# Block-recurrent cross attention and SwiGLU on one core: batch 0's exponentials transposed unnormalised, read states turned one batch later, orders dealt anew

## The chip, the core and the metric

The kernel runs on one core of a Trainium2 chip. A core has five engines, each of which works through its own list of instructions in order: PE (TensorE, matrix products and transposes), DVE (VectorE), ACT (ScalarE), POOL (GpSimd) and SP (SyncE, which here only issues DMA transfers). They share an on-chip buffer, SBUF, and PE writes its results to PSUM, a small accumulator memory of eight banks, from which another engine reads them. Engines wait for each other by semaphores.

The metric is the device time of one execution in microseconds, the median of several runs. What can be told from no change is about 0.2%.

## The reference

Everything is float32. Attention between tokens `x` (8 batches, 8 heads, 512 tokens, 64 wide) and a small `state` (32 rows per head) runs both ways, and a feed-forward network follows over the 512 + 32 rows of each batch:

```python
scores = x @ state.T / 8                 # per batch and head: 512 x 32
a = exp(scores - scores.max(-1)); a /= a.sum(-1) + 1e-9
xread = a @ state                        # 512 x 64
scores2 = state @ x.T / 8                # 32 x 512
a2 = exp(scores2 - scores2.max(-1)); a2 /= a2.sum(-1) + 1e-9
sread = a2 @ x                           # 32 x 64
x = concatenate([xread, sread])          # heads side by side: (8 * 544) x 512
xn = x / sqrt(mean(x * x) + 1e-6) * rms_g
out = (silu(xn @ w_gate) * (xn @ w_val)) @ w_out      # 512 -> 1536 -> 512
```

## The kernel before

**The fold.** `xread` is never formed for the tokens. Since `xn @ w` is (a times state) times w, the kernel multiplies each head's state with the weights first (`own_weights`, L708: products at L721, copies to SBUF as `v` at L733), and the FFN's first product becomes `v` against the transposed attention weights `aT_s`. The mean square that the norm needs comes from the same weights: in batch 0 through the Gram matrix of the state, later from the squares of the read (L447, L457). `mean_root` (L306, on POOL) turns it to the inverse root `ri`, `along_rows` (L312, transposes at L316) lays `ri` along the tokens, and a DVE product puts it into `aT_s`.

**Batches.** Batch 0's tokens take the plain products: `hidden` (L753) for each of twelve blocks m of 128 hidden columns, 128x512 with two contraction steps for the gate and two for the value, then silu on ACT and the gated product on DVE, then `project_as_ready` (L964). From batch 1 on, products go by a seven-product scheme over halves: `hidden_seven` (L858, products at L868) and `project_twice` (L1141, products at L1172, copies of parts `kept` at L1185, their sums on DVE L1212 and POOL L1200 to L1205, stores at L1288). They take sums of `v` (`vs`, POOL L748 to L751) and of `aT_s` (`aT_t`, `slot_sums`, L782). The 256 state rows of all batches come last, from the collected `xsT`.

**Softmax of batch 0.** It goes in two halves of 256 tokens. `half_read` (L540) sums the exponentials, divides by the sum, transposes the result to `aT_s` (PE L555, ACT L558), forms the Gram product (L562), multiplies it with `aT_s` (L566), sums over partitions with a product by a column of ones (L571), and scales by `ri`.

**The read of the states.** `states_read` (L602) does the second softmax. For batches 2 and later its exponentials go through DRAM and come back transposed; PE forms the read `rp` (L656, small tiles 128*32, bank `at`), ACT scales it to `sr` (L672), PE transposes `sr` (L675), and ACT copies that to `xsT` (L677).

**What sets the order.** Each part is a Python generator, a stream, and a string of letters says which stream takes its next step: `ORDER` for batch 0, `FIRST` for batch 1, `PERIOD` for batches 2 to 6, `LAST` for batch 7, `STATES` for the end. The instructions of all five engines are then in exactly that order. In the later strings `a` is the next batch's `tokens_read`, `s` its `states_read`, `w` its first `own_weights` products, `x` copies of `v`; `h`, `t`, `u` are the hidden products, their copies and sums; `p`, `c`, `k`, `o` are the projection's products, copies, sums and stores; `f`, `g`, `l` are loads. So near the end of each period, the next batch's softmax is finished among the projection's products. I call that place the seam.

**PSUM.** The banks are in pools: `aps` (two, name `at`), `vps` (two, `pv`), `fx` (two), `fy` and `fz` (one each, all named `f`). A product must wait until the last reader of the bank that it takes is done.

Some products use a part of PE's array (the profile's 64*32, 128*32 and 32*64 behind the name); the text calls runs of them small-tile groups, and the others dense.

Of the kernel before, what the change touches and what calls it, by code (L numbers as in the profile page):

```python
# [8 lines left out]
F32 = mybir.dt.float32  # L9
# [5 lines left out]
ALU = mybir.AluOpType  # L15
# [11 lines left out]
    "zzzzaazagaaigaagaazzzebzaaaaabgdabbebbeessbbbzaaddsbbbAeAaadbAaabdAbbeAAAadbAAAb"  # L27
    "aabvdbbevvedAhteeieeAAAhuhtAddssddssppihvvivupAssAAdssshssAAtpseeeddhushedspeedd"
    "AAAApAAdAtvvvhhhuptuheeeddpppeeeddhdvtueeAApeAAdvvedddpAAASdAAeedhtedhuhtvAvvpSS"
    "SAAApSSSSSehuehthAAeeeehuAeppSddpdddvdvvhtudSSkkkkkhkkQkkkQQhhttphQQQuuQQQppppck"  # L30
    "kQQQcAApcwwwwwwwwpwcSS"
# [3 lines left out]
    "vhhththtuhhhuthutataaaaaahhthhluhuxhxxhvvuuuhttuthhhxxxxxthxhhuuauuhaaftauukkktk"  # L35
    "htthhhvauutuuahththxxxhthaaauaahhhhuuuutttasuhhthhhppusuuuauutuauuhukkkkgukaappp"
    "pppskpcppppppppkkkkkfffckkkkakkgpcakkaaakpppcosagaggggspppppppapppapcssckkkaakkk"
    "kaaaaasssoppppkoolaappkppkppppsaapappkkkkoaafwsswcpssfxxsxpcoowxxox"
# [3 lines left out]
    "hahtqqtavaxqaaxhthahhahuuvvtqhuuhthttqxxxqhqqqquGhhhuutxquhhuqafthathhatxxaxuhhq"  # L42
    "qquuhtuhqththhthhuukukkuutvkxxuuahtthaaahhhaafxsthuuuutsuhthahhtuuuuaahhtuuthupp"
    "hsssauaGffpgppcpppGluukukkkpckkppkkkkppkpkkkapapppppaacppppkckkpppakpppagakaaacp"
    "ggsskppaaaookpgkkaakpakagkkckkaoopasppklpkpkpksssppaasfpppasskooappcssawwgwxxfxx"
    "xxpcoo"
)
LAST = (
    "vhhtfthhthxuhguxhtvvhutuhxfhtuthuhhuhhxtuthfxhtuxtxuhxhuhuvtauhhhthxuuthkxthuhhh"
    "kuututxhxtkhuhhthuuuuhututhhhutuhhutguuthukpuphuuukpppkpkgpckpkppkkakppkppkppkpc"  # L50
    "pkakpppkpkckpkkkpakpcppkkacpopppppppakcokkpkpkkkgppkappapkggkakpppppcfopkopgcooo"
    "ao"
# [8 lines left out]
def kernel(  # L61
# [124 lines left out]
    VE.memset(blocks, 0.0)  # L186
    for j in range(4):
        VE.memset(blocks[Ns * j:Ns * j + Ns, Ns * j:Ns * j + Ns], 1.0 / DM)

# [350 lines left out]
    def half_read(h):  # L540

        eS, aT = soft_0["e"][:, HT * h:HT * h + HT], aT_s[0][:, :, HS * h:HS * h + HS]
        e = eS.rearrange("p c e j n -> p (c e j) n")
        z = soft_0["z"][:, HT * h:HT * h + HT].rearrange("p c k -> p (c k)")
        VE.reduce_sum(out=z, in_=e, axis=AXX)
        yield
        VE.tensor_scalar(z, z, 1e-9, None, op0=ALU.add)
        VE.reciprocal(z, z)
        yield
        VE.tensor_tensor(out=e, in0=e, in1=z.unsqueeze(2).to_broadcast(e.shape), op=ALU.mult)  # L550
        yield
        tp = aps.tile([P, 2, HT, P], F32, name="at")
        for i in range(2):
            for c in range(HT):
                TE.transpose(out=tp[:, i, c, :], identity=ident,  # L555
                             in_=eS[:, c, i].rearrange("p j n -> p (j n)"))
        yield
        SE.copy(aT, tp.rearrange("p e c t -> p e (c t)"))  # L558
# [24 lines left out]
        yield  # L583
# [18 lines left out]
    def states_read(b):  # L602
# [48 lines left out]
        rp = aps.tile([P, 2, D], F32, name="at")  # L651
# [21 lines left out]
        yield  # L673
        tp = aps.tile([P, 4, Ns], F32, name="at")
        TE.transpose(out=tp.rearrange("p j n -> p (j n)"), in_=sr, identity=ident)  # L675
# [77 lines left out]
    def hidden(m, lhs, rhs):  # L753
# [6 lines left out]
        def products():  # L760
            for k, to in enumerate((gp, vp)):
# [571 lines left out]
    soft_0["z"] = two.tile([P, NC, 2 * 4], F32, name="z1")  # L1333
    aT_s[0] = two.tile([P, 2, S], F32, name="aT_s")
# [20 lines left out]
    with tc.manual_schedule(**by_hand):  # L1355
# [7 lines left out]
        for b in range(1, B):  # L1363
# [56 lines left out]
```

## Time and profile before

| | |
|---|---|
| median of 3 runs | 741.5 us (741.49 to 742.0) |
| the profiled execution | 741.17 us, of which the span of instructions is 739.1 us |
| PE, DVE, ACT, POOL busy | 99%, 77%, 50%, 36% of the span |
| granted PE clock | 1.0 |
| mean DMA rate | 198 GB/s |

A row of the timeline reads: start, length, engine and line, operation, out<-in, tile of PE's array, shape and number of records; in brackets the idle time ahead of it and what ended it. PE writes two records for most float32 matmuls, and one for a transpose. Ends of PE's records are modelled and overlap the next start, so the distance between starts is the better price. A row of the windows reads: stretch, its length, then for PE, weight loads, DVE, ACT and POOL the busy time and the number of instructions, then PE's clock, the share of DMA time and GB/s.

### The profile page before, as it was taken

To read this page: it belongs to the slowest core of one execution; us is meant where nothing else is said; L and a number is where in the kernel's file an instruction comes from. 1 tells how busy PE (TensorE), PEld (TensorE's weight loads), DVE (VectorE), ACT (ScalarE), POOL (GpSimd) and SP (SyncE) were. 2 spreads that over 40 slices of the span, in tenths; PEclk is the share of its full clock that TensorE was granted. 3 is DMA by queue.
4 is the path that set the end of the run, shared out by engine and by line. 5 is a ranking of instruction groups with operands and counts; after the bars stand their busy time and mean duration, and the time that the engine had idled before them with its cause. 6 is when DMAs were issued, how large, how long until landed. Compare 5 with 4: busy or idle time off the path is not lost.

```text
span 739.1 us, 14234 instructions
## 1 busy us (share of the span) xinstructions
PE 732.8 (99%) x5588; PEld 589.5 (80%) x5588; DVE 565.9 (77%) x943; ACT 367.5 (50%) x620; POOL 264.6 (36%) x360
## 2 busy tenths in 40 slices
PE   8999999999999999999999999999999999999998
PEld 7543444889878997799888987899779987899996
DVE  5775577999848994699569984899569955788862
ACT  5997843563365526472366336552557236511220
POOL 2300004512474127412761247412741277325400
PEclk9999999999999999999999999999999999999999
DMA  8978846973782478418870768238840873063411
GB/s 238 371 279 317 339 175 255 300 279 104 220 308 58 179 255 287 135 34 312 264 242 6 279 202 316 60 147 276 298 131 21 322 228 112 1 226 116 137 51 28
DMA packets 58426, 146.15 MB, mean 198 GB/s; under 512 B 10228, under 2 KB 29176, under 8 KB 51448
## 3 DMA queue, kind: packets, MB, share of 16 engines
q1 hardware_dynamic: 47312, 126.30, 48.1%
q10 hardware_dynamic: 11048, 18.95, 9.0%
q8 instruction: 44, 0.72, 0.4%
q14 instruction: 22, 0.18, 0.1%
HBM read 116.46 MB, written 28.77 MB: 197 GB/s over the span
## 4 chain that ended last, share of the span: by engine, by line
PE 73%; DVE 19%; issue 3%; ACT 2%; POOL 2%; DVEq 0%; POOLq 0%
PE f L868 37%; PE f L1172 10%; PE f L971 6%; PE pv L764 6%; PE pv L721 4%; PE at L721 3%; PE f L1034 2%; DVE hb L1231 2%; DVE h L1220 2%; DVE h L1222 2%; DVE h L1226 2%; DVE sq L457 2%; DVE kept L1212 1%; PE at L656 1%; DVE h L1224 1%
## 5 line engine op out<-in xcount | busy, mean ns | idle before, releaser
L868 PE MATMUL f<-aT_s,v 128*128 128x256 f32 x504 | 119.0, 382 | 0.0
L868 PEld LDWEIGHTS f<-aT_s,v 128*128 128x128 f32 x504 | 94.7, 190 | 22.7 <-issue 5.3
L931 DVE TENSOR_TENSOR g<-g,f 128x512 f32<-128x512 f32 x84 | 55.9, 684 | 60.5 <-PE f L868 51.1
L1200 POOL TENSOR_TENSOR kept<-kept 128x256 f32<-128x256 f32 x28 | 22.7, 810 | 194.1 <-DVE kept L1212 180.6
L1185 ACT COPY kept<-f 128x512 f32<-128x512 f32 (+1 forms) x56 | 29.7, 531 | 119.8 <-PE f L1172 93.8
L868 PE MATMUL f<-aT_t,vs 128*128 128x256 f32 x336 | 86.8, 382 | 0.0
L1172 PE MATMUL f<-w,h 128*128 128x128 f32 x588 | 74.9, 277 | 0.0
L868 PEld LDWEIGHTS f<-aT_t,vs 128*128 128x128 f32 x336 | 62.9, 190 | 13.5 <-issue 2.8
L1172 PEld LDWEIGHTS f<-w,h 128*128 128x128 f32 x588 | 70.0, 192 | 4.1 <-issue 4.1
L922 ACT ACTIVATE hb<-g 128x1024 f32<-128x1024 f32 x42 | 44.5, 1060 | 50.6 <-DVE g L931 50.3
L748 POOL TENSOR_TENSOR vs<-v 128x256 f32<-128x256 f32 x42 | 31.1, 740 | 97.3 <-ACT v L733 97.1
L944 DVE TENSOR_TENSOR hb<-hb,f 128x512 f32<-128x512 f32 (+1 forms) x48 | 31.1, 649 | 23.7 <-PE f L868 23.7
L971 PE MATMUL f<-wo,hb 128*128 128x512 f32 x96 | 44.1, 599 | 0.0
L944 DVE TENSOR_TENSOR hb<-hb,c 128x512 f32<-128x512 f32 (+1 forms) x48 | 37.6, 782 | 8.3 <-ACT hb L922 7.3
L764 PE MATMUL pv<-aT_s,v 128*128 128x512 f32 x96 | 43.9, 597 | 0.0
L868 PE MATMUL f<-aT_t,v 128*128 128x256 f32 x168 | 43.7, 382 | 0.0
L868 PE MATMUL f<-aT_s,vs 128*128 128x256 f32 x168 | 43.1, 379 | 0.0
L1172 PE MATMUL f<-wo,h 128*128 128x128 f32 x336 | 42.1, 275 | 0.0
L1172 PE MATMUL f<-wo,hb 128*128 128x128 f32 x336 | 42.1, 275 | 0.0
L1172 PEld LDWEIGHTS f<-wo,hb 128*128 128x128 f32 x336 | 40.3, 192 | 0.4
L309 POOL TENSOR_TENSOR ri<-ss,mhalf 128x4 f32<-128x4 f32 (+1 forms) x9 | 9.7, 1078 | 86.1 <-ACT ss L397 71.6
L1172 PEld LDWEIGHTS f<-wo,h 128*128 128x128 f32 x336 | 39.8, 192 | 0.0
(230 smaller groups left out, 1593.1 us busy)
## 6 DMA issues: line engine op xcount, KB each, us to landing
w_m<-w_d SPq DMA_DIRECT2D x48, 1024.0 KB
w<-t_d SPq DMA_DIRECT2D x49, 576.0 KB
out_dram<-kept SPq DMA_DIRECT2D x28, 256.0 KB
raw<-in_moe_w_val_dram SPq DMA_DIRECT2D x6, 1024.0 KB
raw<-in_moe_w_out_dram SPq DMA_DIRECT2D x6, 1024.0 KB
w_d<-w_m SPq DMA_DIRECT2D x6, 1024.0 KB
x_b<-in_x_dram SPq DMA_DIRECT2D x6, 1024.0 KB
x_d<-xB ACTq DMA_DIRECT2D x6, 1024.0 KB
```

The costliest lines, as they stand in the source:

```text
L457: VE.tensor_tensor(out=sq[:, i, :], in0=sq[:, i, :], in1=sq[:, j, :], op=ALU.add)
L721: TE.matmul(out=pv[e][Ns * j:Ns * j + Ns, :], lhsT=stT_g[b][D * e:D * e + D, j, :], rhs=w[D * e:D * e + D, j].rearrange("p m k f -> p (m k ...
L748: GE.tensor_tensor(out=vs[:, 0], in0=a21, in1=a22, op=ALU.add)
L764: TE.matmul(out=to[0], lhsT=lhs(i, k), rhs=r, start=(i == 0), stop=(i == len(rhs) - 1))
L868: TE.matmul(out=ps[:, i, 0:half], lhsT=l[:, i, :], rhs=r, start=(start and i == 0 and k == 0), stop=(k == len(lhs) - 1), skip_group_check= ...
L922: SE.activation(out=hb[:, 2 * mp:2 * mp + 2, 0:n].rearrange("p m (c t) -> p m c t", c=2), in_=q["g"][:, :, :, 0:half], func=ACTF.Silu if s ...
L931: VE.tensor_tensor(out=to, in0=to, in1=q[ps][:, :, 0:half], op=ALU.add)
L944: VE.tensor_tensor(out=part, in0=part, in1=val, op=ALU.mult)
L971: TE.matmul(out=banks[r], lhsT=hb[:, m, P * r:P * r + P], rhs=wo[:, m, :], start=(m == 0), stop=(m == NM - 1))
L1172: TE.matmul(out=to[half][:, slot, :], lhsT=lhs[:, k, :], rhs=rhs[:, k, :], start=(fresh and n in (0, 4) and k == 0), stop=(k == QM - 1), s ...
L1185: SE.copy(of_half(k, i), banks[name][i])
L1200: GE.tensor_tensor(out=k[:, 4:8:3], in0=k[:, 5:6].to_broadcast([P, 2, QD]), in1=k[:, 4:8:3], op=ALU.add)
```

## The change

It has four parts.

1. `half_read` transposes batch 0's exponentials as they are, directly behind the exponential (L549 of the changed file). The sum, its reciprocal and the reciprocal's square `zz` (POOL) are formed beside that; the normalised copy is a new tile `en`. The Gram product and the squares are taken of the unnormalised values; the sums over partitions come out per head (a product with the four columns of `of_head`), are multiplied by `zz` into `qz`, whose ninth column holds 1e-6, and are added up. Then `en` is transposed into the same `aT_s`. For each half this is four PE transposes, one ACT copy, one DVE operation and one POOL operation more. `ri` is laid along the tokens in the bank fz instead of pv.
2. The first block of `hidden` (m = 0) makes its products in token halves: eight of 256 columns instead of four of 512, so that the first four need only the first half of `aT_s`.
3. For batches 2 and later the state's read goes to fz, and the transpose of `sr` with its copy becomes a stream of its own, `states_turned` (letter `n`), in the next batch's string.
4. The strings `ORDER`, `PERIOD`, `FIRST` and `LAST` are new; `STATES` is not.

```diff
 PERIOD = (
-    "vhhththtuhhhuthutataaaaaahhthhluhuxhxxhvvuuuhttuthhhxxxxxthxhhuuauuhaaftauukkktk"
...
+    "vxahthththuhuhuthththhthhvvhaaaxxhhxxafaauuuutttuhhthhaahhuuuuttxhuhhthhauukkath"
...
     def half_read(h):
...
-        VE.reduce_sum(out=z, in_=e, axis=AXX)
-        yield
-        VE.tensor_scalar(z, z, 1e-9, None, op0=ALU.add)
-        VE.reciprocal(z, z)
-        yield
-        VE.tensor_tensor(out=e, in0=e, in1=z.unsqueeze(2).to_broadcast(e.shape), op=ALU.mult)
-        yield
         tp = aps.tile([P, 2, HT, P], F32, name="at")
...
         SE.copy(aT, tp.rearrange("p e c t -> p e (c t)"))
         yield
+        z, zz = (soft_0[k][:, HT * h:HT * h + HT].rearrange("p c k -> p (c k)") for k in ("z", "zz"))
+        VE.reduce_sum(out=z, in_=eS.rearrange("p c e j n -> p (c e j) n"), axis=AXX)
+        yield
+        VE.tensor_scalar(z, z, 1e-9, None, op0=ALU.add)
+        VE.reciprocal(z, z)
+        GE.tensor_tensor(out=zz, in0=z, in1=z, op=ALU.mult)
+        yield
+        en = x_0.tile([P, HT, 2, 4 * Ns], F32, name="en")
+        e = eS.rearrange("p c e j n -> p (c e j) n")
+        VE.tensor_tensor(out=en.rearrange("p c e (j n) -> p (c e j) n", n=Ns), in0=e,
+                         in1=z.unsqueeze(2).to_broadcast(e.shape), op=ALU.mult)
+        yield
         ga = vps.tile([P, 2, HS], F32, name="pv")
...
-        sp = fy.tile([P, HT], F32, name="f")
+        sp = fy.tile([P, HT, 2, 4], F32, name="f")
         for i in range(2):
             for c in range(HT):
-                TE.matmul(out=sp[:, c:c + 1], lhsT=sq[:, i, P * c:P * c + P], rhs=ones,
-                          start=(c == 0 and i == 0), stop=(i == 1), skip_group_check=True)
-        yield
+                TE.matmul(out=sp[:, c, i, :], lhsT=sq[:, i, P * c:P * c + P], rhs=of_head,
+                          start=True, stop=True)
+        yield
+        qz = soft_0["qz"][h]
+        VE.tensor_tensor(out=qz[:, :, 0:2 * 4], in0=sp.rearrange("p c e j -> p c (e j)"),
+                         in1=soft_0["zz"][:, HT * h:HT * h + HT], op=ALU.mult)
         ss = two.tile([P, NC], F32, name="ss")
-        VE.tensor_scalar(ss[:, 0:HT], sp, 1e-6, None, op0=ALU.add)
+        VE.reduce_sum(out=ss[:, 0:HT], in_=qz, axis=AXX)
         yield
         ri = mean_root(ss[:, 0:HT], HT)
         yield
-        rp = along_rows(ri, HT, vps, "pv")
+        tp = aps.tile([P, 2, HT, P], F32, name="at")
+        for i in range(2):
+            for c in range(HT):
+                TE.transpose(out=tp[:, i, c, :], in_=en[:, c, i, :], identity=ident)
+        yield
+        SE.copy(aT, tp.rearrange("p e c t -> p e (c t)"))
+        yield
+        rp = along_rows(ri, HT, fz, "f")
...
-        rp = aps.tile([P, 2, D], F32, name="at")
+        rp = aps.tile([P, 2, D], F32, name="at") if b < 2 else fz.tile([P, 2, D], F32, name="f")
...
+        unturned[b] = sr
+        if b < 2:
+            yield from states_turned(b)
+
+    unturned = {}
+
+    def states_turned(b):
+
         tp = aps.tile([P, 4, Ns], F32, name="at")
-        TE.transpose(out=tp.rearrange("p j n -> p (j n)"), in_=sr, identity=ident)
+        TE.transpose(out=tp.rearrange("p j n -> p (j n)"), in_=unturned.pop(b), identity=ident)
...
         def products():
+            if m == 0:
+                gp.append(vps.tile([P, S], F32, name="pv"))
+                vp.append(vps.tile([P, S], F32, name="pv"))
+                for t in (slice(0, HS), slice(HS, S)):
+                    for k, to in enumerate((gp, vp)):
+                        for i, r in enumerate(rhs):
+                            TE.matmul(out=to[0][:, t], lhsT=lhs(i, k), rhs=r[:, t],
+                                      start=(i == 0), stop=(i == len(rhs) - 1))
+                    yield
+                return
...
+            if b > 1:
+                streams.update(n=states_turned(b))
```

On PE at the start of the program, from the first half's transposes of the exponentials (`eS`) to the first gate products (`pv<-aT_s,v`). Before:

```order
L592 MATMUL at<-xT,apart 32x256 x16
L1312 MATMUL f<-wake 128x256
L555 MATMUL at<-ident,eS 128x128 x4
L327 MATMUL at<-ident,rows 128x128
L562 MATMUL pv<-aT_s,gram 128x256 x2
L555 MATMUL at<-ident,eS 128x128 x4
...
L316 MATMUL pv<-ident,ri 128x128 x2
L721 MATMUL f<-w_m,stT_g 32x512 x8
L316 MATMUL pv<-ident,ri 128x128 x2
L365 MATMUL at<-xT,stT 32x512 x8
L764 MATMUL pv<-aT_s,v 128x512 x6
```

After:

```order
L549 MATMUL at<-ident,eS 128x128 x4
...
L608 MATMUL at<-xT,apart 32x256 x16
L1346 MATMUL f<-wake 128x256
L568 MATMUL pv<-aT_s,gram 128x256 x2
...
L549 MATMUL at<-ident,eS 128x128 x4
L577 MATMUL f<-of_head,eS 128x4 x4
L591 MATMUL at<-ident,en 128x128 x4
...
L319 MATMUL f<-ident,ri 128x128 x2
L745 MATMUL f<-w_m,stT_g 32x512 x8
L368 MATMUL at<-xT,stT 32x512 x8
L319 MATMUL f<-ident,ri 128x128 x2
L791 MATMUL pv<-aT_s,v 128x256 x8
```

The first half's transposes stand ahead of the states' scores, those of `en` are new (the second half's are among the rows left out), and the two small-tile groups L745 and L368 now stand side by side.

On PE at the seam into batch 4, the end of period 3 (`part` holds the group sums for the norm, `x_b,e` is the read of the states, `w_m,stT_g` are the next batch's `own_weights`; numbers behind a name tell buffers apart). Before:

```order
L392 MATMUL at<-part,groups 128x16
L1172 MATMUL f<-w_2950,hb 128x128 x3
L1172 MATMUL f<-w_2950,h_3061 128x128 x6
L316 MATMUL at<-ident,ri 128x128 x4
L656 MATMUL at<-x_b,e_2783 32x64 x32
L721 MATMUL pv<-w_m,stT_g 32x512 x8
L1172 MATMUL f<-wt,h_3061 128x128 x3
L675 MATMUL at<-ident,sr 128x128
L1172 MATMUL f<-wt,h_3061 128x128 x3
L721 MATMUL at<-w_m,stT_g 32x512 x8
L721 MATMUL pv<-w_m,stT_g 32x512 x8
L868 MATMUL f<-aT_s,v 128x256 x2
```

After:

```order
L395 MATMUL at<-part,groups 128x16
L1206 MATMUL f<-wt,hb 128x128 x3
L1206 MATMUL f<-w_3016,hb 128x128 x3
L1206 MATMUL f<-w_3016,h_3115 128x128 x6
L1206 MATMUL f<-wt,h_3115 128x128 x3
L319 MATMUL at<-ident,ri 128x128 x4
L1206 MATMUL f<-wt,h_3115 128x128 x3
L745 MATMUL pv<-w_m,stT_g 32x512 x8
L745 MATMUL at<-w_m,stT_g 32x512 x8
L672 MATMUL f<-x_b,e_2812 32x64 x32
L745 MATMUL pv<-w_m,stT_g 32x512 x8
L330 MATMUL at<-ident,rows 128x128
```

The group sums stand one group of three matmuls further ahead, one more group stands between them and the transposes of `ri`, and the two small-tile groups have become one. The seam of batch 1 before has three such groups (L656 alone, L721 twice, L721 once) and after the change one, in the same order as here. In batches 2 to 6, the transpose L330 of the next state's rows also stands here now.

On ACT at the same seam (`ss` is read from the group sums). Before:

```order
L397 ACTIVATE ss<-at,bounds 32x4 x4
L1185 COPY kept<-f 128x512
L672 ACTIVATE sr<-at,z_2786 128x64 x2
L733 COPY v<-pv 128x512 x2
L677 COPY xsT<-at 128x4x32
L1185 COPY kept<-f 128x384
L733 COPY v<-at 128x512 x2
```

After:

```order
L400 ACTIVATE ss<-at,bounds 32x4 x4
L757 COPY v<-pv 128x512 x2
L757 COPY v<-at 128x512 x2
L1219 COPY kept<-f 128x512
L1219 COPY kept<-f 128x384
L688 ACTIVATE sr<-f,z_2815 128x64 x2
L757 COPY v<-pv 128x512
L949 COPY g<-f 128x2x256
```

The scaled read `sr` is taken behind four copies of `v` and two of `kept`, where one copy of `kept` stood ahead of it. On SP the load of the next `x_b`, which overwrites what the read of the states takes, is issued behind that read as before.

More of the change, by code (lines that the diff above doesn't have):

```diff
@@ L26 @@
 ORDER = (
[L27 to L31, printed above, removed]
+    "zzzzaazaaaaggggaaazzzbzeeeaaabddaaabbeeddbbbbsssbzaaaAAAAabbdbeaaaaabAbbbAAAAAdb"
+    "bbbaavAAbbbsevvsheddhtuededdeAehhAAtsAupdppsevsvvAAApessssAAhsAAAAsddAdsAhhtueee"
@@ L39 @@
+    "xxxhhvuuakktuhutththhxxxhuahhaauaaauuuugtthssghuuuutthhhuutfunaauupphuuppkppppnp"
+    "plskkkkkpppkkkkgpckackkkpaaapppppffpakkkksppppppakaaakacccppppgpsassgooapkkkkkca"
+    "aappkkaaskosspppppppsaaapaaaggkppakkkkkpppooaapwwwxflxxoxxxcsscfsoo"
 )
 FIRST = (
-    "hahtqqtavaxqaaxhthahhahuuvvtqhuuhthttqxxxqhqqqquGhhhuutxquhhuqafthathhatxxaxuhhq"
-    "qquuhtuhqththhthhuukukkuutvkxxuuahtthaaahhhaafxsthuuuutsuhthahhtuuuuaahhtuuthupp"
-    "hsssauaGffpgppcpppGluukukkkpckkppkkkkppkpkkkapapppppaacppppkckkpppakpppagakaaacp"
@@ L45 @@
-    "ggsskppaaaookpgkkaakpakagkkckkaoopasppklpkpkpksssppaasfpppasskooappcssawwgwxxfxx"
-    "xxpcoo"
+    "aaaaahtvvqqqqqqqqahathhhvtuqquxxhhtqhuhxqthutthuuhhaaahauxttqhtfuxxxhhqqhhthxuuu"
+    "qhuhuhttuukavtkahhtxkhaaaahhhuuuhtttkGhGxGhxuuuutsuxhuhuthththaaauhhhthauppuuuut"
+    "auahauuupppppppgkafffkukkkkkgcppppppppagkkkkpcppppaakoalggpaaaakaakkkkskaakscpap"
+    "csakkssspppppppccppkgpppgopaaakkasapkkkkppppppkkppokkkksoooaasppswwwfxxxxxxcclfo"
+    "soss"
 )
 LAST = (
-    "vhhtfthhthxuhguxhtvvhutuhxfhtuthuhhuhhxtuthfxhtuxtxuhxhuhuvtauhhhthxuuthkxthuhhh"
@@ L50 @@
-    "kuututxhxtkhuhhthuuuuhututhhhutuhhutguuthukpuphuuukpppkpkgpckpkppkkakppkppkppkpc"
-    "pkakpppkpkckpkkkpakpcppkkacpopppppppakcokkpkpkkkgppkappapkggkakpppppcfopkopgcooo"
-    "ao"
+    "vhhtnfthhnthxuhguxhtvvhutuhxfhtuthuhhuhhxtuthfxhtuxtxuhxhuhuvtauhhhthxuuthkxthuh"
+    "hhkuututxhxtkhuhhthuuuuhututhhhutuhhutguuthukpuphuuukpppkpkgpckpkppkkakppkppkppk"
+    "pcpkakpppkpkckpkkkpakpcppkkacpopppppppakcokkpkpkkkgppkappapkggkakpppppcfopkopgco"
+    "ooao"
 )
@@ L186 @@
     VE.memset(blocks, 0.0)
+    of_head = x_0.tile([P, 4], F32, name="of_head")
+    VE.memset(of_head, 0.0)
     for j in range(4):
         VE.memset(blocks[Ns * j:Ns * j + Ns, Ns * j:Ns * j + Ns], 1.0 / DM)
+        VE.memset(of_head[Ns * j:Ns * j + Ns, j:j + 1], 1.0)
     w_d = [scratch.tile([P, NI, 2, 2, P], F32, name="w_d%d" % mp) for mp in range(NM // 2)]
@@ L1333 @@
     soft_0["z"] = two.tile([P, NC, 2 * 4], F32, name="z1")
+    soft_0["qz"] = [x_0.tile([P, HT, 2 * 4 + 1], F32, name="qz%d" % h) for h in range(2)]
+    for qz in soft_0["qz"]:
+        VE.memset(qz, 1e-6)
+    soft_0["zz"] = x_0.tile([P, NC, 2 * 4], F32, name="zz")
     aT_s[0] = two.tile([P, 2, S], F32, name="aT_s")
```

8 lines of the change are left out of this document (3 added, 5 removed).

## The prediction

> **What bounds the kernel now.** I read the page first, then the view of waits on TensorE (PE), then the windows by stage, then the instruction timeline at the two places that the change rewrites: the start and the seam between two batches.
>
> ```profile
> span 739.1 us, 14234 instructions
> ...
> PE 732.8 (99%) x5588; PEld 589.5 (80%) x5588; DVE 565.9 (77%) x943; ACT 367.5 (50%) x620; POOL 264.6 (36%) x360
> ```
>
> ```profile
> PE at L327 <- ACT aT_s L558: 0.7, 1, 0.7
> PE at L555 <- ACT sS L599: 0.2, 1, 0.2
> ```
>
> ```profile
> 26.70:75.00 48.30, 48.30 (x241) 20.54 (x234) 33.50 (x52) 43.18 (x53) 2.32 (x6) 1.00 0.84 314
> ...
> 325.00:359.00 34.00, 34.00 (x306) 32.94 (x304) 33.34 (x58) 12.07 (x27) 8.12 (x9) 1.00 0.67 237
> ```
>
> PE is busy for 99% of the span at a granted clock of 1.00 (the column after the engines, in the window rows). The view of waits shows, beside one wait at the very start, only the two above, both in batch 0's softmax. So another engine's work is free unless PE comes to wait for it, and the sum is one of PE's own records and stalls. The window rows also show where the cover is thin: ACT is busy for 43.18 of 48.30 us in batch 0's FFN, DVE for 33.34 of 34.00 us before a seam.
>
> A seam (the one into batch 4; start, length, line, out<-in, records) shows PE's costs that the waits don't:
>
> ```profile
> 355.46 1.50 PE L1172 MATMUL f<-wt,hb 128*128 128x128 f32 x12
> 356.80 0.29 PE L392 MATMUL at<-part,groups 128*128 128x16 f32 x2
> ...
> 357.70 1.50 PE L1172 MATMUL f<-w,h 128*128 128x128 f32 x12
> 359.34 0.65 PE L316 MATMUL at<-ident,ri 128*128 128x128 f32 x4
> 359.92 1.10 PE L656 MATMUL at<-x_b,e 128*32 128x64 f32 x64
> 360.95 1.09 PE L721 MATMUL pv<-w_m,stT_g 64*32 64x512 f32 x16
> 361.97 0.94 PE L1172 MATMUL f<-wt,h 128*128 128x128 f32 x6
> 362.74 0.27 PE L675 MATMUL at<-ident,sr 128*128 128x128 f32 x1
> 362.85 0.83 PE L1172 MATMUL f<-wt,h 128*128 128x128 f32 x6
> 363.62 1.09 PE L721 MATMUL at<-w_m,stT_g 64*32 64x512 f32 x16
> 364.50 1.06 PE L721 MATMUL pv<-w_m,stT_g 64*32 64x512 f32 x16
> 365.49 1.13 PE L868 MATMUL f<-aT_s,v 128*128 128x256 f32 x4
> ```
>
> Lengths overlap, so I price by the distance between starts. A 128x128 record takes 1.34 / 12 = 0.112 us (355.46 to 356.80), and a transpose 0.11 (362.74 to 362.85). Two costs stand out. First, twelve records from 357.70 would end at 359.04, and the next group starts at 359.34: a stall of 0.30. Second, small-tile groups (64*32, 128*32) cost at their edges: six dense records take 0.77 behind such a group (361.97 to 362.74) and 0.77 ahead of one (362.85 to 363.62) where 0.67 is their pace, so 0.10 at each edge; and L721 takes 0.88 when another L721 follows (363.62 to 364.50), 0.99 when a dense group follows (364.50 to 365.49).
>
> The stall is a chain: group sums on PE (356.80), then ss on ACT, then ri on POOL, for which L316 waits.
>
> ```profile
> 357.13 1.06 ACT L397 ACTIVATE ss<-at,bounds 32x4 f32<-32x4 f32 x4 [6.23 <-DMA e<-e_d]
> ```
>
> ```profile
> 358.27 1.02 POOL L309 TENSOR_TENSOR ri<-ss,mhalf 128x4 f32<-128x4 f32 x1 [1.40 <-ACT ss L397]
> ```
>
> ri ends at 359.29, and L316 starts at 359.34. It recurs: five seams stall, of which the first and the last are
>
> ```profile
> 277.77 1.17 PE L1172 MATMUL f<-w,h 128*128 128x128 f32 x9
> 279.09 0.65 PE L316 MATMUL at<-ident,ri 128*128 128x128 f32 x4
> ...
> 598.57 1.39 PE L1172 MATMUL f<-w,h 128*128 128x128 f32 x11
> 600.10 0.54 PE L316 MATMUL at<-ident,ri 128*128 128x128 f32 x3
> ```
>
> Nine records from 277.77 end at 278.78, eleven from 598.57 at 599.80: 0.31 and 0.30 of stall.
>
> **The change, part by part.** *Seams of batches 2 to 6 (five).* The group sums move ahead of six more records, 0.67 us earlier, and three matmuls (six records) of the next product stand ahead of the transposes of ri, so 30 records lie between where 18 did. ri would be ready 2.54 us after the sums as now (356.80 to 359.34), at 358.67; PE arrives at 356.13 + 0.15 + 30 x 0.112 = 359.63. The stall of 0.30 goes, with 0.96 to spare. The sums' input from DVE comes behind the same thirteen DVE operations as before. Gain 0.30, between 0 (DVE late, first rival) and 0.31.
>
> Also here two small-tile groups become one. Before: 2.05 (359.92 to 361.97) and 1.87 (363.62 to 365.49), with four edges of 0.10: 4.32. After, in its order L745, L745, L672, L745: 0.88, then the second at 0.99 if leaving for L672 costs like leaving for dense work, 1.03 (L656 to L721 now, 359.92 to 360.95), 0.99, and two edges: 4.09. If leaving for L672 is free, 3.98; if it costs an edge more, 4.19. So 0.23, bounds 0.13 and 0.34; I take 0.20, toward the dearer end, since all that ends an L721 run in these rows costs. Seams: 5 x (0.30 + 0.20) = 2.5.
>
> The Trainium skill, page TensorEngine Tiling (Array Packing), section Tiling Modes, speaks against part of this: changing the tiling mode drains the array, so the merged group (two modes, 64*32 and 128*32) still changes inside, four changes where there were five. With the rows' 0.10 for one edge that makes 0.10 a seam, and the sum 0.5 us higher. The trace agrees that edges cost; no row has L721 followed by L656.
>
> *The transpose of sr one batch later* is one transpose there instead of here, 0.11 either way, and its copy on ACT moves with it. In the last batch it adds one transpose to a batch without a seam: nothing on balance. *The state read's product moves to the bank fz*, which batch b+1's own products need next. ACT's reads of it now stand behind four copies:
>
> ```profile
> 361.65 0.52 ACT L672 ACTIVATE sr<-at,z 128x64 f32<-128x64 f32 x2 [2.46 <-DVE z L649]
> ...
> 364.80 1.07 ACT L733 COPY v<-at 128x512 f32<-128x512 f32 x2 [0.59 <-PE at L721]
> ...
> 366.70 0.58 ACT L915 COPY g<-f 128x512 f32<-128x512 f32 x1 [0.84 <-POOL vs L749]
> ```
>
> On PE, L672 would end at about 363.7 (359.63 + four transposes and six records 1.12 + edge 0.10 + 0.88 + 0.99 + 1.03). On ACT the second pair of v copies can start when the second L745 ends, 362.7, and ends 1.07 later at 363.8; two copies of kept of about 0.53 (the sr pair's and the g copy's rows bound it: 0.52, 0.58) bring 364.9, the sr pair 365.4. PE needs fz after the third L745 (0.99), an edge (0.10), the transpose of rows (0.11) and the first two L902 matmuls (four records of 128x256, twice as wide as a 128x128 record and so about 0.22 each: 0.87), at about 365.8. Slack 0.4: no cost, but it is the thinnest cover here. The x_b load stands behind the later state read as well:
>
> ```profile
> 361.08 0.38 SPq L138 DMA_DIRECT2D x_b<-in_x_dram  x1
> ```
>
> ```profile
> 371.77 1.89 DVE L348 STREAM_TRANSPOSE xB<-x_b 128x512 f32<-128x512 f32 x3
> ```
>
> It would be issued 2.7 later (363.8) and has until 371.8: 8 us against the 10.7 it has now; taken as hidden.
>
> *Seam of batch 1.* There is no stall of ri to win, and three small-tile groups become one: 2 x 0.20 = 0.4 (0.2 to 0.7).
>
> *Batch 0's start.* On PE:
>
> ```profile
> 14.46 1.13 PE L592 MATMUL at<-xT,apart 64*32 64x256 f32 x32
> 15.52 0.70 PE L1312 MATMUL f<-wake 128*128 128x256 f32 x2
> 16.38 0.66 PE L555 MATMUL at<-ident,eS 128*128 128x128 f32 x4 [0.16 <-ACT sS L599]
> 17.71 0.33 PE L327 MATMUL at<-ident,rows 128*128 128x128 f32 x1 [0.68 <-ACT aT_s L558]
> ...
> 25.34 0.43 PE L316 MATMUL pv<-ident,ri 128*128 128x128 f32 x2
> 25.70 1.09 PE L365 MATMUL at<-xT,stT 64*32 64x512 f32 x16
> 26.72 3.70 PE L764 MATMUL pv<-aT_s,v 128*128 128x512 f32 x8
> ```
>
> From 14.46 to the first gate product at 26.72 are 12.26 us. The first four transposes of eS go ahead of 14.46 (the exponentials need no division now), so L608 starts at 14.90 and those 0.44 leave the stretch. The eight transposes of en come in: 8 x 0.11 = 0.88. The waits of 0.16 and 0.68 have their transposed half long done: -0.84. L745 and L368 stand side by side, one group's edges less: -0.2. The rest of the head (gram, the four-column sums) has as many records. 14.90 + 12.26 - 0.44 + 0.88 - 0.84 - 0.20 = 26.56; small stalls round the two waits can go too: 15.52 to 16.38 holds 0.86 for two 128x256 records, which take 0.44 at that pace, so 0.26 beyond the 0.16. That gives 26.3. What could take it back is ACT:
>
> ```profile
> 24.69 1.30 ACT L265 ACTIVATE lin<-raw,bounds 128x1024 f32<-128x1024 int16 x1
> 25.87 1.08 ACT L733 COPY v<-f 128x512 f32<-128x512 f32 x2
> ...
> 28.01 1.28 ACT L770 ACT_TABLE_LOAD   x1
> 29.31 0.60 ACT L770 ACTIVATE t<-pv 128x512 f32<-128x512 f32 x1
> ```
>
> v is copied behind a 1.30 us conversion and two added copies (0.58 each, as the g copy above) precede it; v ends at 26.95 now. Gain 0.4: the one end is 1.2 (both waits, all small stalls and the token halves hiding the second half's ri), the other -0.3 (both added copies not hidden, against the waits). The token halves are the same columns: eight of 256 for four of 512, no cost beyond rounding. DVE's added operations and POOL's zz lie beside this work.
>
> *The rest of batch 0* is dealt anew: the same products, the same number of small-tile groups, and ACT loads its tables twelve times less over the program (20 for 32, 1.28 each), which is cover in the window where it is busy 43.18 of 48.30. New stalls are bounded by 0 and by the nearest row, the 0.68 that PE once waited for an ACT copy: I take 0.2.
>
> Sum: 741.17 (the profiled execution; 739.1 is its span) - 2.5 - 0.4 - 0.4 + 0.2 = 738.1. The median of the runs, 741.5, stands 0.33 above that execution: **738.5**.
>
> **The rivals.** (1) *DVE takes the stall over.* With 33.34 of 34.00 us busy it can't follow a PE that runs 0.5 us ahead; group sums or the hidden sums come late by what ri gave. For: the row. Against: PE waits nowhere for DVE there now. The 1.5 returns and some of the edges: 740.2.
> (2) *Slower: fz.* If ACT's pair of sr comes later than summed, PE's first product into fz waits at all six seams. From 0.4 late it costs; from 1.15 late (0.75 x 6 = 4.5) the kernel is slower than before by over 0.2%; at 1.5 late 738.5 + 6 x 1.1 = 745.1. For: four copies ahead of it in an in-order queue, each bound to a product or a free bank. Against: ACT idles 6.23 and 2.46 us in the rows above.
> (3) *Start without gain:* the new transposes and copies cost what the waits gave: 738.5 + 0.4 + 0.3 = 739.2.
> (4) *Every change of tile kind costs an edge,* inside the merged group too: 0.10 a seam instead of 0.20, with batch 1 at 0.2: 739.2. This is the drain of the page named above.
>
> **How the numbers follow.** 0.2% is 1.5 us, about what a measurement of this kernel can tell from no change: same is 740.0 to 743.0. Chances: forecast 0.45 (its own range 736.9 to 740.0, from the bounds of start and edges), rival 4 0.14, rival 3 0.09, rival 1 0.14 (a fifth of it below 740.0), rival 2 0.18. Faster 0.45 + 0.14 + 0.09 + 0.03 = 0.71, same 0.11, slower 0.18. The range goes from 736.9, with 0.05 below, up into rival 2 to 743.5, with 0.15 above.
>
> **What would show it.** After: each seam's L319 follows its records without a gap, and the periods shorten from about 80.25 (279.09 to 600.10 is 321.01 in four) by 0.5; six dense records of L1206 ahead of one small-tile group; the first L791 at about 26.3, no wait on aT_s at 17.7. Wrong would be a wait of L902 on sr at the seams (rival 2), waits on DVE's h or part (rival 1), or of L791 on v (rival 3).

## The result: 738.37 us, and the profile after

The changed kernel takes 738.37 us (median of 9 runs, 737.84 to 738.78), where the kernel before took 741.5 beside it. The ratio is 0.9948, with a 95% interval from 0.9931 to 0.9965: faster by half a per cent. The forecast was 738.5. A few executions of any of these kernels take some microseconds longer than the rest (here one of the nine before, 746.72), and a median that holds several of them says less than the traces.

The page after has the same shape as before: PE at 99%, and DVE, ACT and POOL about as busy as they were.

```profile
span 736.5 us, 14288 instructions
...
PE 730.9 (99%) x5604; PEld 591.4 (80%) x5604; DVE 564.6 (77%) x952; ACT 350.2 (48%) x610; POOL 271.4 (37%) x362
```

The view of waits on PE has lost the two waits of batch 0's softmax and shows another there, for a load of x (the first row is the wait at the very start, which the kernel before has too):

```profile
PE f L1346 <- DVE wake L155: 1.1, 1, 1.1
PE at L522 <- DMA x_b<-in_x_dram: 0.5, 1, 0.5
```

The windows by stage show that DVE is still nearly full ahead of a seam, but a little less than before (32.59 for 33.34 of 34.00 us):

```profile
325.00:359.00 34.00, 34.00 (x308) 32.93 (x307) 32.59 (x58) 11.72 (x27) 9.81 (x11) 1.00 0.71 246
```

And this is the timeline of PE at the seam into batch 4, whose rows of before the prediction shows:

```profile
354.63 0.83 PE L1206 MATMUL f<-wt,hb 128*128 128x128 f32 x6
355.34 0.37 PE L395 MATMUL at<-part,groups 128*128 128x16 f32 x2
355.55 0.92 PE L1206 MATMUL f<-wt,hb 128*128 128x128 f32 x6
...
358.31 0.83 PE L1206 MATMUL f<-wt,h 128*128 128x128 f32 x6
358.98 0.60 PE L319 MATMUL at<-ident,ri 128*128 128x128 f32 x4
359.42 0.83 PE L1206 MATMUL f<-wt,h 128*128 128x128 f32 x6
...
360.18 1.09 PE L745 MATMUL pv<-w_m,stT_g 64*32 64x512 f32 x16
361.06 1.06 PE L745 MATMUL at<-w_m,stT_g 64*32 64x512 f32 x16
362.06 1.10 PE L672 MATMUL f<-x_b,e 128*32 128x64 f32 x64
363.09 1.09 PE L745 MATMUL pv<-w_m,stT_g 64*32 64x512 f32 x16
364.11 0.33 PE L330 MATMUL at<-ident,rows 128*128 128x128 f32 x1
364.27 1.03 PE L902 MATMUL f<-aT_s,v 128*128 128x256 f32 x4
365.14 2.08 PE L902 MATMUL f<-aT_t,vs 128*128 128x256 f32 x8
```

The six records from 358.31 take 0.67 and L319 follows at 358.98 without a gap. L745, left for L672, takes 1.00 (361.06 to 362.06), as much as it takes when left for dense work. Behind the group stands a single transpose, of 0.16, and then L902 runs at its pace (0.87).

Where the time went, by the starts of the same groups in the two profiled executions (rows of the timeline; the last column is counted from the start of the program):

| place on PE | before | after | gained up to here |
|---|---|---|---|
| first gate product | 26.72 | 26.50 | 0.22 |
| first hidden product of batch 1 | 123.92 | 123.80 | 0.12 |
| of batch 2 | 204.98 | 204.72 | 0.26 |
| of batch 3 | 285.24 | 284.50 | 0.74 |
| of batch 4 | 365.49 | 364.27 | 1.22 |
| of batch 5 | 445.75 | 444.05 | 1.70 |
| of batch 6 | 526.00 | 523.82 | 2.18 |
| of batch 7 | 606.25 | 603.43 | 2.82 |
| last group of matmuls | 732.69 | 729.87 | 2.82 |

So each of the five periods from batch 2 to batch 7 is 0.48 shorter (the last 0.64, since no transpose of the next rows stands there), 2.56 in all, and the rest of the program gives 0.26. The extra 0.16 of the last is work that moved and not work that went: batch 0 ends with the first of these transposes now. The seams themselves give 5 x 0.48 = 2.4.

Below, the first half of a batch reaches from its first hidden product to its last group of them (`f<-aT_t,v`, at 325.73 in batch 3), and the rest is called from middle to seam. Of the 0.48, from middle to seam gives 0.42 (38.55 for 38.97), and the next first half 0.06 (41.23 for 41.29).

### The profile page after: what moved, and what is told of

The parts are those of the page before. It is cut to its first block, busy times and chain, and to the rows that moved or that the text cites. A ratio compares the mean times of both kernels' runs of the same rounds, so it can differ in the third digit from the quotient of the medians.

```text
span 736.5 us, 14288 instructions
## 1 busy us (share of the span) xinstructions
PE 730.9 (99%) x5604; PEld 591.4 (80%) x5604; DVE 564.6 (77%) x952; ACT 350.2 (48%) x610; POOL 271.4 (37%) x362
## 4 chain that ended last, share of the span: by engine, by line
PE 98%; DMA 1%; SPq 0%; issue 0%; ACT 0%
PE f L902 40%; PE f L1206 31%; PE f L1005 6%; PE pv L798 5%; PE pv L745 4%; PE f L1068 2%; PE at L745 2%; DMA x_b<-in_x_dram 1%; PE at L450 1%; PE f L672 1%; PE at L368 1%; PE pv L791 0%; PE at L319 0%; PE at L672 0%; PE f L577 0%; PE pv L529 0%
## 5 line engine op out<-in xcount | busy, mean ns | idle before, releaser
L902 PE MATMUL f<-aT_s,v 128*128 128x256 f32 x504 | 118.8, 381 | 0.0
L902 PEld LDWEIGHTS f<-aT_s,v 128*128 128x128 f32 x504 | 94.9, 191 | 19.3 <-issue 5.3
L1234 POOL TENSOR_TENSOR kept<-kept 128x256 f32<-128x256 f32 x28 | 24.4, 872 | 171.5 <-DVE kept L1246 112.7
L902 PE MATMUL f<-aT_t,vs 128*128 128x256 f32 x336 | 86.7, 382 | 0.0
L902 PEld LDWEIGHTS f<-aT_t,vs 128*128 128x128 f32 x336 | 62.6, 190 | 13.2 <-issue 3.1
L772 POOL TENSOR_TENSOR vs<-v 128x256 f32<-128x256 f32 x42 | 33.0, 785 | 106.7 <-ACT v L757 106.5
L954 ACT COPY g<-f 128x512 f32<-128x512 f32 x42 | 24.6, 585 | 49.0 <-PE f L902 49.0
L757 ACT COPY v<-pv 128x512 f32<-128x512 f32 x56 | 31.0, 595 | 31.9 <-PE pv L745 31.6
L902 PE MATMUL f<-aT_t,v 128*128 128x256 f32 x168 | 43.8, 383 | 0.0
L902 PE MATMUL f<-aT_s,vs 128*128 128x256 f32 x168 | 43.2, 380 | 0.0
L965 DVE TENSOR_TENSOR c<-c,f 128x512 f32<-128x512 f32 (+1 forms) x48 | 31.2, 650 | 15.1 <-PE f L902 15.0
```

The source lines that it names most:

```text
L757: SE.copy(v[:, e].rearrange("p m k f -> p (m k f)"), pv[e])
L772: GE.tensor_tensor(out=vs[:, 0], in0=a21, in1=a22, op=ALU.add)
L902: TE.matmul(out=ps[:, i, 0:half], lhsT=l[:, i, :], rhs=r, start=(start and i == 0 and k == 0), stop=(k == len(lhs) - 1), skip_group_check= ...
L954: SE.copy(gates(q)[1], q["x"][:, :, 0:half])
L965: VE.tensor_tensor(out=to, in0=to, in1=q[ps][:, :, 0:half], op=ALU.add)
```

## The experiments

The first two runs take the change apart by place.

**Batch 0 alone.** The later strings and the state's read are those of before:

```diff
-PERIOD, FIRST, LAST of the changed kernel
+PERIOD, FIRST, LAST of the kernel before
-        rp = aps.tile([P, 2, D], F32, name="at") if b < 2 else fz.tile([P, 2, D], F32, name="f")
+        rp = aps.tile([P, 2, D], F32, name="at")
...
-        if b < 2:
-            yield from states_turned(b)
+        yield from states_turned(b)
```

> Only batch 0 is changed (half_read, token halves, ORDER); the later strings, the bank of the states' read and its transpose are those of before. My theory: the gain sits at the seams, so this keeps only the start's 0.2 (first gate product at 26.5 for 26.72) and the five seams stall for 0.30 again: 741.3 (741.0 to 741.6), periods of 80.25. Rival (batch 0's new order carries the gain, by freeing ACT of twelve table loads): below 740.

It took 741.2, where the kernel before took 741.66 beside it (ratio 1.0001, interval 0.9986 to 1.0016): no gain that can be measured. The first gate product stood at 26.75 rather than 26.5, as PE had waited 0.78 for x there. The seams of batches 2 to 5 had their old spacing of 80.26, and ri stalled as before (twelve records from 277.58 end at 278.92, L319 at 279.23). That the gain sits at the seams held; the 0.2 of the start was not seen in this run.

**The seams alone.** Batch 0 is that of before, the later strings and `states_turned` are the new ones:

```diff
-PERIOD, FIRST, LAST of the kernel before
+PERIOD, FIRST, LAST, states_turned and the bank fz of the changed kernel
```

> Only the later strings, the bank fz and the transpose one batch later are changed; batch 0 is that of before. My theory: 741.5 less about 2.5 for batches 1 to 6, so 738.8 (738.4 to 739.2), first gate product at 26.72, periods of 79.8. Rival (batch 0 carries the gain): above 740.5.

It took 746.07, beside 741.66 for the kernel before (ratio 1.0067, interval 1.005 to 1.0083), a miss of 7 us. From batch 2 on all was as expected (79.79 a period), but batch 1's first half took 48.97 where it takes 42.22 before and 42.38 after. The view of waits and the windows name the place:

```profile
PE f L876 <- ACT c L926: 3.9, 1, 3.9
...
PE at L729 <- DVE w L1134: 1.0, 1, 1.0
```

```profile
129.00:134.00 5.00, 1.56 (x8) 1.03 (x6) 4.14 (x7) 0.30 (x1) 1.06 (x2) 1.00 0.72 293
134.00:140.00 6.00, 5.57 (x29) 2.97 (x30) 3.37 (x5) 2.81 (x5) 3.71 (x4) 0.72 0.58 216
```

```profile
133.25 0.41 ACTq L350 DMA_DIRECT2D x_d<-xB  x1
133.70 0.59 ACT L926 COPY c<-f 128x512 f32<-128x512 f32 x1 [7.51 <-DVE xB L348]
```

```profile
124.63 0.29 DVE L685 COPY xsT<-at 128x128 f32<-128x128 f32 x1 [4.29 <-PE at L683]
```

The old ORDER ends with the transpose of batch 1's `sr` on PE and its copy on DVE. The new ORDER has both some 25 us earlier (the transpose at 98.71 in the trace after). The new FIRST has eight sums of weights and the transposes of x early on DVE, so with the old ORDER they all stood behind that copy, for which DVE sat idle for 4.29; ACT stood 7.51 behind DVE for its transfer of x, and PE behind ACT. (In the kernel before, DVE sits idle for 4.30 ahead of the same copy, but the old FIRST has little on DVE behind it, and PE doesn't wait.) The two strings are one plan, and half of it costs more than the whole change gives. Behind the stall the granted clock was 0.72 on average from 134 to 140 (0.50 from 136 to 139), and the 4.8 us of waits came to a loss of 6.6.

**The seams of batches 2 to 6 alone.** So the cut was moved by one batch: ORDER and FIRST are those of before.

```diff
-FIRST of the changed kernel
+FIRST of the kernel before, less its last two letters s
```

> Only PERIOD and LAST are the changed ones, with the bank fz and the later transpose; batch 0 and batch 1 are those of before (FIRST without its last two steps of s). The run with seams only had lost 6.6 us in batch 1's first half, where the new FIRST put weight sums on DVE that the old ORDER had placed elsewhere. My theory (the strings of batches 0 and 1 hang together, the seams of 2 to 6 stand alone): no such loss, periods of 79.8, 741.5 less 5 x 0.47 = 739.1 (738.7 to 739.6). Rival (the seams' gain needs batch 0's change too): above 740.5.

Its profiled execution took 739.31, within the forecast; the median of its ten runs, 739.93 (739.22 to 745.38), lies 0.3 above the forecast's range, and the ratio of 0.9964 (0.9924 to 1.0004) alone wouldn't tell it from the kernel before. The trace does: its periods were 79.79. The seam of batch 1 took 0.59 longer than before, since the read of the states now takes fz, and the old FIRST has it before DVE's last sums have read that bank:

```profile
198.56 1.10 PE L656 MATMUL f<-x_b,e 128*32 128x64 f32 x64 [0.44 <-DVE kept L1220]
```

So the five seams give without the rest what they give in the whole change.

**ri late again.** In PERIOD the group sums stand three matmuls later and the transposes of ri three earlier:

```diff
-aaaggkppakkkkkpppooaapwww
+aggkpaapakkkkkppaaooppwww
```

> The changed kernel, but in batches 2 to 6 the group sums stand three matmuls later and the transposes of ri three matmuls earlier, so that 18 records lie between them as before the change; the merged small-tile group stays. My theory: the stall of 0.30 returns at five seams, less about 0.1 each that the group sums now wait for DVE: 738.4 + 5 x 0.2 = 739.4 (739.1 to 739.9), and PE stands about 0.3 ahead of ri at each seam. Rival (the gain is all in the merged groups, the stall was only a gap in the records): 738.4.

One run, 740.28, 0.4 above the forecast's range. Four seams were 0.25 longer than in the changed kernel (38.80 for 38.55 from middle to seam), and one 0.83. The first two rows show the usual stall (twelve records from 277.17 end at 278.51, and L319 starts at 278.82), the third the long one:

```profile
277.17 1.50 PE L1206 MATMUL f<-w,h 128*128 128x128 f32 x12
278.82 0.65 PE L319 MATMUL at<-ident,ri 128*128 128x128 f32 x4
```

```profile
359.44 0.65 PE L319 MATMUL at<-ident,ri 128*128 128x128 f32 x4 [0.72 <-POOL ri L312]
```

In the long one ACT issued the four transfers of e until 357.18 and could start on ss, behind them in its queue, only then; in the trace after, ss starts as soon as the group sums are there. So the stall was real, worth 0.25 net of what the group sums win, and without cover it can be 0.8. The rival that the stall was a mere gap in the records, and so costs nothing, is out.

**The merged group split.** Three dense matmuls move into it:

```diff
-aapwwwxflxxoxxxcss
+aawwwxflxxopxxxcss
```

> The changed kernel, but in batches 2 to 6 three dense matmuls stand inside the merged small-tile group, ahead of the states' read. My theory (each side of a dense group next to a small-tile group costs about 0.10): 0.20 a seam, 738.4 + 1.0 = 739.4, ri still without a stall. Rival (every change of tile kind costs 0.10, inside the group too, so a split adds only one change): 0.10 a seam, 738.9. Rival (the gain is all in ri): 738.4.

One run, 742.08: 0.73 a seam, more than either theory had. The rows show why:

```profile
360.09 1.09 PE L745 MATMUL pv<-w_m,stT_g 64*32 64x512 f32 x16
360.97 1.59 PE L745 MATMUL at<-w_m,stT_g 64*32 64x512 f32 x16
362.49 0.94 PE L1206 MATMUL f<-wt,h 128*128 128x128 f32 x6
363.36 1.10 PE L672 MATMUL f<-x_b,e 128*32 128x64 f32 x64
```

```profile
360.20 1.22 DVE L463 TENSOR_TENSOR aT_s<-aT_s,at 128x1024 f32<-128x1024 f32 x1 [1.37 <-PE at L319]
```

The second L745 takes 1.52 instead of 1.00, as it needs the bank `at` that DVE reads until 361.42. In taking the dense matmuls from between L319 and the group, the edit had also taken their cover. The dense six took 0.87, 0.20 over their pace. So it was run again with three matmuls left in that place:

```diff
-pppooaapwwwxflxxoxxxcss
+ppooaapwwwxflxxopxxxcss
```

> The changed kernel, but three dense matmuls stand inside the merged small-tile group as in the split run, taken from ahead of the transposes of ri, so that three others still stand between ri and the group. In the split run the group also waited 0.5 for DVE's product with ri, which reads the bank that L745 takes. My theory: that wait goes and the split alone costs 0.20 a seam, 738.4 + 1.0 = 739.4. Rival (only a change of tile kind costs): 0.10 a seam, 738.9.

One run, 739.13, with an early start (first gate product at 26.08). Every seam was 0.20 longer than in the changed kernel (38.75 for 38.55), and the group held no other stall:

```profile
360.22 1.06 PE L745 MATMUL at<-w_m,stT_g 64*32 64x512 f32 x16
361.22 0.94 PE L1206 MATMUL f<-wt,h 128*128 128x128 f32 x6
362.08 1.10 PE L672 MATMUL f<-x_b,e 128*32 128x64 f32 x64
```

0.20 is the edge theory's number, not the 0.10 of the rival. Yet the rule behind that rival, of the Trainium skill, page TensorEngine Tiling (Array Packing), section Tiling Modes, holds as far as it goes: a change of the mode costs inside the group too, L745 taking 1.00 ahead of L672 and 0.88 ahead of another L745. What was wrong was to give every change the same price. By these rows it is 0.12 from one small-tile kind to the other, 0.10 into a group, and 0.11 and 0.10 out of one (on its last run and on the first dense records). What L672 pays when it is left for L745 stays open, as no row has it left for another L672.

**The bank fz.** ACT writes `sr` three times over:

```diff
-        for e in range(2):
+        for e in (0, 1) * (1 if b < 2 else 3):
             to, z = sr[:, D * e:D * e + D], z2[:, e:e + 1]
```

> The changed kernel, but for batches 2 to 7 ACT writes the scaled read sr three times over, which holds the bank fz and ACT's queue about 0.82 longer at six seams. The profile after shows sr done at 364.89 and PE's first product into fz at 365.14, so a slack of 0.25. My theory: PE waits for 0.82 - 0.25 = 0.57 at each, 738.4 + 6 x 0.57 = 741.8 (741 to 743). Rival (the bank or ACT's queue has more cover than that): 738.4.

One run, 743.11, just above the forecast's range: 0.70 at each of six seams. The view puts the wait down to POOL, but POOL's vs (L773) had ended at 367.09, and ACT's sr ended at 367.34, 0.10 ahead of PE:

```profile
367.44 2.11 PE L902 MATMUL f<-aT_t,vs 128*128 128x256 f32 x8 [0.51 <-POOL vs L773]
```

```profile
366.00 1.34 ACT L688 ACTIVATE sr<-f,z 128x64 f32<-128x64 f32 x6
```

0.8 more of ACT cost 0.70, so the slack in the changed kernel is about 0.1: the 0.25 between the rows less what passes between ACT's end and PE's start. The slower rival of the prediction was a real mechanism, and the change passes it by a tenth of a microsecond.

**Group sums later.** They go back to their old place, and the transposes of ri stay:

```diff
-aaaggkppakkkkkpppooaapwww
+aggkpaapakkkkkpppooaapwww
```

> The changed kernel, but in batches 2 to 6 the group sums stand three matmuls later, where they stood before the change; the transposes of ri stay. My theory: PE loses about 0.1 at the group sums now, since DVE's part ends 0.15 before them; that goes, and ri, ready about 2.7 after the sums, still comes ahead of PE: 738.4 - 5 x 0.1 = 737.9. Rival (the margin is gone and ri stalls again): 738.4 to 739.4.

One run, 740.82, a miss where 737.9 was forecast. The 0.12 at the group sums was won (38.43 for 38.55 from middle to seam), and ri did not stall. But behind three of the five changed seams the first half of the next batch took 41.48 instead of 41.23, and in the last batch 40.70 instead of 40.32; behind the fifth, where PE had just waited 0.6 for a transfer of e, it took 41.23:

```profile
365.98 2.08 PE L902 MATMUL f<-aT_t,vs 128*128 128x256 f32 x8
368.05 1.13 PE L902 MATMUL f<-aT_s,vs 128*128 128x256 f32 x4
```

```profile
367.28 0.72 POOL L775 TENSOR_TENSOR vs<-v,vs 128x256 f32<-128x256 f32 x1
```

L902 starts at 368.05 as POOL's last sum of the first v ends at 368.00. POOL has ri, four sums of kept, four of aT_t and four of vs in one unbroken row, so a ri that comes 0.67 later moves all of it. Neither theory had this; the net is a loss of about 0.14 a period. Most of the rest of that run's time is a late load of x at the start (PE waited 1.33) and the one late transfer of e (0.6).

**The token halves.** The first block takes its columns at once, as before (`if m < 0` for `if m == 0`):

> The changed kernel, but the first block of hidden products takes all 512 columns at once as before. My theory (the halves hide the second half of the tokens): PE waits for the second half of aT_s, ready at 27.66, where the first product stood at 26.50, so the time goes up by about 1.1, to 739.5. Rival (the copies of v, which end at 26.9, bind the start either way): up by at most 0.4, 738.4 to 738.8.

One run, 739.17, and the wait is there:

```profile
25.86 0.43 PE L319 MATMUL f<-ident,ri 128*128 128x128 f32 x2
27.45 4.96 PE L798 MATMUL pv<-aT_s,v 128*128 128x512 f32 x11 [1.16 <-DVE aT_s L597]
```

The halves hide 1.16 us of the second half's scaling, which stands behind a transpose of eS on DVE. The copies of v don't bind.

**x first.**

```diff
     load_x_half(0)
-    load_piece(0)
     load_x_half(1)
+    load_piece(0)
```

> The changed kernel, but the second half of batch 0's x is loaded ahead of the first piece of the weights. PE waits 0.54 for that half now, and the first gate product came 0.2 later than forecast. My theory: that wait is the missing 0.2; without it the first gate product comes at 26.1 to 26.3 and the time falls by 0.2 to 0.4, to 738.1. Rival (another engine binds the start: weights that land later, or the exponentials): no gain, or a loss of up to 1.

One run, 740.05, a miss where 738.1 was forecast. The wait for x went, and a longer one came, as the weights' first piece landed later and ACT, in order, took its conversions ahead of the exponential:

```profile
13.16 0.66 PE L549 MATMUL at<-ident,eS 128*128 128x128 f32 x4 [1.36 <-ACT eS L540]
```

```profile
10.35 0.78 ACT L268 ACTIVATE lin<-raw,bounds 128x512 f32<-128x512 int16 x1 [2.69 <-DMA raw<-in_moe_w_gate_dram]
```

The first gate product stood at 27.36, 0.86 later than in the changed kernel: the rival was right. Another 0.7 of that run is one seam at which a transfer of e came late.

**g ahead of v on ACT.** An attempt at the last 0.10 that PE loses on its second product of a batch:

```diff
-vxahththth
+vahtxhthth
```

> The changed kernel, but at the seams of 2 to 6 ACT copies the first hidden product (g) ahead of the third copy of v. PE's second product stands at 366.11 in the profile after, 0.10 later than its pace, since g ends at 365.96. My theory: it loses that 0.10, and up to 0.07 at the third: 738.4 - 5 x 0.12 = 737.8. Rival (the third copy of v, now 0.6 later, reaches POOL's sums of v too late): slower, 738.4 to 741.

The changed kernel itself stood beside it, on the same chip:

> The changed kernel itself, beside the runs above on their chip: 738.4 (737.8 to 738.8).

It took 738.83 (737.94 to 739.34), 0.46 more than in its first nine runs, and the edited one 739.46 (739.25 to 740.48), where 737.8 was forecast: slower by 0.11 a period (first halves of 41.35 for 41.23).

```profile
364.82 0.52 ACT L688 ACTIVATE sr<-f,z 128x64 f32<-128x64 f32 x2
365.83 0.59 ACT L949 COPY g<-f 128x512 f32<-128x512 f32 x1 [0.50 <-issue]
366.32 0.59 ACT L757 COPY v<-pv 128x512 f32<-128x512 f32 x1
366.79 0.60 ACT L952 COPY c<-f 128x512 f32<-128x512 f32 x1
```

g starts 1.11 after its product does (364.72), with v ahead of it or not, so it gained nothing. The copy of v had been filling that gap, and now it delays c.

## Why the prediction was right, and where its sizes were off

**The bound.** PE was the bound and stayed it, and a sum of its records and stalls could forecast the change. That 738.5 lies only 0.13 from the median is in part luck. The terms of the sum add up to 3.1 (so 738.4, where the prediction wrote 738.5), and the starts on PE show 2.82: the seams of 2 to 6 gave nearly what was forecast, while batch 1 and the start together gave 0.44 less. The medians lie further apart (3.13) than the profiled executions (2.74), as the median before stands 0.33 above its profiled execution and the one after 0.06 below. And the median of the same kernel in the last run above was 0.46 higher.

**Seams of 2 to 6: 2.5 forecast, 2.4 measured** (2.56 with the transpose that moved). The stall of ri was put at 0.30; undoing it cost 0.25, since the earlier group sums have a price: six records ahead of them and their own two take 0.92 (354.63 to 355.55), 0.11 over the old rows' pace, because DVE's input comes just then (DVE's reduction to `part` at L392 runs from 354.50 to 355.19, and L395 starts at 355.34). The prediction said that the thirteen DVE operations stand as before and left out that PE arrives earlier. The merged group was put at 0.23 and taken as 0.20; the split measured 0.20. That L745 pays when left for L672 was the uncertain step, and at 1.00 it was taken rightly (0.99). The two experiments account for 0.45 of the 0.48.

**Seam of batch 1: 0.4 forecast.** From batch 1's first product to batch 2's the gain was 0.14. Its first half took longer, 42.38 for 42.22, though the transpose of the rows had left it for the end of batch 0. The rows there show small stalls of 0.07 to 0.10 at three products (starts at 126.63, 128.53 and 134.17). The sum had no term for a first half that FIRST deals anew, and what these products wait for stays open. The seam itself gave 0.30. There 0.20 for each of two groups was too much, since L656 alone stood ahead of the transposes of ri and not of dense matmuls:

```profile
198.16 1.10 PE L656 MATMUL at<-x_b,e 128*32 128x64 f32 x64
199.19 0.65 PE L316 MATMUL at<-ident,ri 128*128 128x128 f32 x4
199.68 0.50 PE L1172 MATMUL f<-w,h 128*128 128x128 f32 x3
```

The six records ahead of it end at 198.07 and the four transposes take 0.49 for 0.44, so its edges show 0.14. And the transpose of rows that now stands at this seam takes 0.16, where that of sr, which left it, takes 0.11.

**Batch 0's start: 0.4 forecast, 0.22 measured.** Here the step "L608 starts at 14.90" failed: it started at 15.16. PE waited for the second half of x,

```profile
11.46 0.63 PE L522 MATMUL at<-ident,x_b 128*128 128x128 f32 x4 [0.54 <-DMA x_b<-in_x_dram]
...
15.16 1.14 PE L608 MATMUL at<-xT,apart 64*32 64x256 f32 x32
...
26.50 3.78 PE L791 MATMUL pv<-aT_s,v 128*128 128x256 f32 x16
```

which it had not in the profiled execution of before. Behind L608 the change gave more than summed: from there to the first gate product it is 12.26 before and 11.34 after, as in every run with the changed start and the token halves (11.33 to 11.36), where the sum had 11.66, or 11.40 with the small stalls gone. What varies is the start of L608, in most of these runs with the landing of x. In the run with the seams alone, whose start is that of before, x was as late (L519 at 11.74) and the first gate product stood at 27.23, 15.49 behind it; after, it is 15.04. In the run with the split group, where PE waited for no x, the changed start reached 26.34, where before had 26.72. Both ways the change is worth about 0.4, as forecast, but single executions scatter by more: the changed kernel's second profile, with no such wait either, has L608 at 15.59 and the first gate product at 26.93, and the run of the seams of 2 to 6, with the old start, had 26.60. So no run shows how much of the 0.4 reaches the median. The size of a landing was missing from the sum.

**The rest of batch 0: a loss of 0.2 taken, 0.10 measured,** and that is the 0.11 of the transpose of rows that moved ahead of the mark: on balance there were no new stalls.

**The rivals.** DVE did not take the stall over, except for the 0.11 at the group sums. Start without gain is out for the stretch behind L608, by the rows above. The slower rival, fz, did not come to pass, but its slack was put at 0.4 and is about 0.1. The rival of tile changes was right that a change inside the group costs, and wrong on the price of what was removed. What the prediction did not name is the row of thirteen POOL instructions behind ri, which would have made the change weaker if ri had not come earlier.

## What to carry to other kernels

When one engine is busy for 99% and its waits add up to nothing, price the gaps between the starts of its groups: a group's pace, its edges and a stall that the records hide are all there, and here they gave the gain of the five seams to a tenth. Where the order was dealt anew without such pricing (batch 1's first half), and where the start hangs on a load, they didn't. A bank or a queue that passes by 0.1 or 0.2 us is no spare room: three of the edits tried here, meant to win a few tenths, ran into the next thing in an in-order queue. And orders that hand work from one stage to the next are one plan: half of it cost 4.4 us where the whole gave 3.

## What the hardware showed unexpectedly

- The same load of x, issued within 0.02 of the same time (from 4.22 or 4.24 on, 1.02 long), released PE's third group of transposes between 11.03 and 12.26 in the seven executions with the changed start and the old order of loads in which PE waited for it, and the first gate product moved with it (26.08 to 27.31). In a kernel whose head hangs on a load, one execution's start can be wrong by 1 us.
- A long stall of PE was followed by an after-price. Behind 4.8 us of waits, 3.9 of them in one piece, the granted clock was 0.72 on average over six microseconds (0.50 from 136 to 139), about 1.8 us more of time. No other execution here shows such a dip, and none has a wait of PE over 1.4 us. That the wait set it off is read from this one trace and was not tested.
- A single transpose right behind a small-tile group took 0.16 in place of 0.11, and the dense products behind it ran at pace, where those six dense records behind a group took 0.10 more.
